# A linear attention that feeds a multiplicative feed-forward block: the first group's x goes straight on chip and its first factors are formed in steps 5 and 6

## The chip, the core and the metric

The kernel runs on one core of a Trainium2 chip. Its engines work side by side, each through its own list of instructions in order, and wait for each other by semaphores: TensorE (PE) multiplies matrices, VectorE (DVE) and ScalarE (ACT) do elementwise work, GpSimd (POOL) small elementwise work and some transfers, SyncE (SP) only issues transfers (DMAs). The metric is the time of one execution on the device in microseconds (us); lower is better.

## The reference

```python
# attention: q, k, v, alpha have the shape (4, 8, 768, 48)
for t in range(S):
    state = alpha[:, :, t, :, None] * state + einsum('bhd,bhe->bhde', k[:, :, t], v[:, :, t])
    y[:, :, t] = einsum('bhd,bhde->bhe', q[:, :, t], state)
x = y.transpose(0, 2, 1, 3).reshape(3072, 384)
# feed-forward: w1, w2 (384, 1024), w3 (1024, 1024), w_out (1024, 384)
out = ((x @ w1) * (x @ w2) @ w3) @ w_out
```

The weights are 64-bit floats in memory and are turned into 32-bit ones on the chip.

## The kernel before

**Two parts.** The first part walks over 24 chunks of 128 positions (4 batches of 6 chunks), one step of the loop `for n in range(N + 1)` for each chunk (L689). The second part (from L787) finishes the feed-forward block. TensorE's products of the feed-forward block (`products`, L515) are put as fill between the attention's work of the first part, and make up nearly all of TensorE's work in the second.

**One step n of the attention.** `load_kq` brings k and q of a later chunk, `load_a` alpha, `load_v` v. `logs` takes the logarithm of alpha, `decays` sums it along the chunk by a product (L340, L343, L346) and takes two exponentials (L349, L350); `decayed` (L359) multiplies k and q by these on VectorE into one of three buffers `qks`. `transposed` turns that with TensorE (L381, an identity matrix as the moving side, 64 rows and 128 columns as weights: two heads of 48 columns, each padded to 64), and ScalarE copies it (L383). `scores` multiplies k and q (L454; from chunk 8 on L430), and VectorE masks the result (L457; L440). `attend_state` (L474) and `attend` (L485, L482) make the chunk's y, which ScalarE copies to `x` (L489); `outer` (L393) and `advance` (L410 to L412, on POOL) carry the state on. In step n the program asks for the scores of chunk n, the transposes of chunk n+1, `attend(n-1)`, `decayed(n+2)` and `decays(n+3)`.

**x on its way to the feed-forward block.** Three chunks make a group of 384 columns, eight groups in all. `attend` puts two stores of x into the queue `later`, and `store` (L305) issues them on SP at the start of the next step, into `xd[g]` in DRAM. `load_x` (L501) reads a group back as `xT` (128 x 3 x 384), and `split_x` makes three parts of it (ScalarE L507, VectorE L508 and L509). For group 0 the load stands in step 4 and the split in step 6.

**Weights.** w1 and w2 come in 128 x 512 pieces (`load_gates`): a load on SP (L236, 512 KB), then the conversion from 64 bits and a split in three parts (L244 to L265), called by `convert` in steps. The first half of the columns takes six pieces, in the order w1, w2, w1, w2, ... The third part of each is formed on TensorE by `third` (L276, L277, L278).

**Gates.** For each group and each 128 of the 1024 columns, `exact` makes the first factor x @ w1 and the second x @ w2 (nine products of 128 x 384 each; L524 and L526 take them out of the result banks), and L563 or L576 multiplies the two. `fill` is a queue of these jobs, and `run(pieces)` calls them between the attention's instructions; one factor is one piece. For group 0 there are eight pieces: five in step 7 and three in step 8.

**What sets the order.** The program's text gives the order for each engine, except that a scheduler may move an instruction of an engine ahead of another that it holds to be later; `after_marks` forbids it to go ahead of the named one. In the order as built, `decayed(n+2)` stands on VectorE ahead of the masks of chunk n in step 4 and ahead of those of chunk 5 in step 5. SP's queue keeps the order of the text. Transfers on it take eight completion semaphores in turn.

**Memory.** `spare` lies in the buffer `x3` that `split_x` writes, and holds alpha of the paired chunks 2 to 7 and two small constant matrices until step 4. `w12` has two tiles, one for each half of the columns.

Of the kernel before, what the change touches and what calls it, by code (L numbers as in the profile page):

```python
# [48 lines left out]
def kernel(  # L49
# [120 lines left out]
    spare = tr[0].tile([C, 3 * KM * TG], FP32R, tag="x3", name="x3")[:].bitcast(FP32)  # L170
    sums2 = spare[:, 0:4 * C].rearrange("p (e s t) -> p e s t", e=2, s=2)
    pairs = [spare[:, ds(4 * C + i * 2 * DM, 2 * DM)].rearrange("p (h s d) -> p h s d", h=H, s=2) for i in range(2)]
# [12 lines left out]

    w12 = [p.tile([C, 3, 2, KM, CW], FP32R, name=f"w12{i}") for i, p in enumerate((w12ap, const))]
# [39 lines left out]
    def to_fp32(*srcs, width=None):  # L226

        n = width or sum(src.shape[1] for src in srcs)
        raw = rawp.tile([C, n], I64, tag="raw", name="raw")
        for i, src in enumerate(srcs):  # L230
            if width:
                rows = ds(i * src.shape[0], src.shape[0])
                to = raw[rows] if len(src.shape) == 2 else raw[rows].rearrange("p (b c) -> p b c", b=src.shape[1])
            else:
                to = raw[:, ds(i * src.shape[1], src.shape[1])]
            nc.sync.dma_start(out=to, in_=src)  # L236
        yield
        words = raw.bitcast(U32).rearrange("p (n w) -> p n w", w=2)
        low, high = words[:, :, 0], words[:, :, 1]

        mant = cvt.tile([C, n], FP32, tag="mant", name="mant")
        top = mant.bitcast(U32)
        rest = cvt.tile([C, n], FP32, tag="rest", name="rest", bufs=2)
        nc.scalar.activation(rest, low, AF.Copy, scale=2.0 ** -52)  # L244
        nc.vector.tensor_scalar(top, high, 0x000FFFFF, 0x00100000, op0=ALU.bitwise_and, op1=ALU.bitwise_or)

        power = cvt.tile([C, n], U32, tag="power", name="power", bufs=2)
        nc.vector.tensor_scalar(power, high, 20, 0x7FF, op0=ALU.logical_shift_right, op1=ALU.bitwise_and)  # L248
        nc.scalar.activation(power, power, AF.Relu, scale=2.0 ** 23, bias=rebias)  # L249
        yield  # L250
        nc.vector.scalar_tensor_tensor(mant, top, 2.0 ** -20, rest, op0=ALU.mult, op1=ALU.add)  # L251
        nc.vector.scalar_tensor_tensor(power, high, 0x80000000, power, op0=ALU.bitwise_and, op1=ALU.bitwise_or)  # L252
        nc.vector.tensor_mul(mant, mant, power.bitcast(FP32))  # L253
        yield
        return mant

    def load_gates(i, kk, half):
        w = yield from to_fp32((moe_w1, moe_w2)[i][ds(kk * C, C), ds(half * CW, CW)])
        h, l, m = (w12[half][:, x, i, kk, :] for x in range(3))
# [110 lines left out]
    def transposed(n):  # L370
# [5 lines left out]
        tp = [bank().rearrange("p (i j c) -> p i j c", i=2, j=NP) for _ in range(2)]  # L376
        for i in range(2):
            for j in range(NP):
                for half in range(2):
                    s = ds(DP * half, DP)  # L380
                    nc.tensor.transpose(tp[half][:, i, j, :], qk[s, i, 2 * j:2 * j + 2, :], ident[s, s])  # L381
        for half in range(2):
            mark["qkT", n] = nc.scalar.copy(qkT[:, :, :, ds(DP * half, DP)], tp[half]).ins  # L383
# [93 lines left out]
    def attend(n):  # L477
# [15 lines left out]
        g, c = divmod(n, G)  # L493
        to = xd[g].rearrange("(b h d) t -> b d h t", b=2, d=D)
        for half in range(2):
            later.append((to[half, :, :, ds(c * C, C)], x[ds(DP * half, D)]))


# [4 lines left out]
    def split_x(g, i):  # L503
        x = st.pop(("xT", g))
# [44 lines left out]
    def factors(g, f):  # L549
        x = [[st["x3", g][:, part, kk, :] for kk in range(KM)] for part in range(3)]  # L550
        half, at = divmod(f * C, CW)
        return [([[w12[half][:, part, i, kk, ds(at, C)] for kk in range(KM)] for part in range(3)], x)
                for i in range(2)]

# [110 lines left out]
    for half in range(DF // CW):  # L665
        for kk in range(KM):
            weights.extend(load_gates(i, kk, half) for i in range(2))
# [17 lines left out]
    FIRST = 6  # L685
# [3 lines left out]
    for n in range(N + 1):  # L689
        store()  # L690
        if n in loads:
            load_x(loads[n])
        if n != 1 and not 2 < n <= FIRST:
            load_a(n + 5)
        raws = (3, 3, 3, 3, 2, 2, 3, 3)[n] if n < 8 else 4
        for m in (n + 3,) * (n <= FIRST) + (n + 4,) * (n >= FIRST):
            load_kq(m)
            if 2 < n <= FIRST and m == n + 3:
                load_a(n + 5)
            if n < FIRST - 2:  # L700
# [17 lines left out]
        if n == FIRST + 1:  # L718
            run(2)
# [3 lines left out]
        if n - 2 in begin and n > FIRST:  # L723
# [3 lines left out]
            fill.extend(gate(g, f) for f in tiles)  # L727
        if n == FIRST:
            with after_marks("l", ("qkT", n + 1)):
                split_x(0, 0)  # L730
            fill.extend(gate(0, f) for f in begin[n - 3][1])
        pieces = ((3, 3, 2, 0) if n > FIRST + 3 else (0, 3, 3, 0))[(n - FIRST) % 4] if n >= FIRST else 0
# [7 lines left out]
        marks = (*[("qkT", n + 1)] * (n < N - 1), *[("qk", n + 1), ("ms", n)] * early, *["x3"] * (n - 2 in begin and n > FIRST))  # L740
        if n < N - 2 and n != FIRST:
# [7 lines left out]
        if n > FIRST:  # L749
# [5 lines left out]
        with after_marks(*[("ms", n)] * (n < 3)):  # L755
            decayed(n + 2)
# [3 lines left out]
        if n == 4:  # L760
            load_x(0)
# [4 lines left out]
        if n <= FIRST:  # L766
# [4 lines left out]
        if n == FIRST:  # L771
            with after_marks("x3", ("e", n + 3)):
                convert(2, raws)
        elif n < N - 2:
            convert(n == FIRST - 1 if early else n % 3 == 0, raws)
        if n == FIRST - 1:
# [97 lines left out]
```

## Time and profile before

| | |
|---|---|
| median of 3 runs | 466.03 us (464.22 to 467.32) |
| profiled execution | 465.8 us, span 464.1 us |
| TensorE busy | 446.0 us, 96% |
| VectorE, ScalarE, GpSimd busy | 371.1 us (80%), 276.3 us (60%), 94.3 us (20%) |
| chain of waits that ends last | PE 87%, DVE 5%, DMA 4%, issue 2%, ACT 1% |
| largest group | L515 `bank<-x,w`, 1152 products, 209.5 us |
| DMA moved | 80.37 MB, 97392 of 148869 packets under 512 bytes |

The span is what the profile's times are measured in; the profiled execution's own time has 1.7 us around it. "Busy" is the time in which an engine works on an instruction; an engine that is not on the chain of waits may be idle at no cost. TensorE's products are pipelined, so one of 337 ns on the page takes about 180 ns of TensorE's time when many follow each other. The chain of waits is followed back from the last instruction, at each step to what released it.

### The profile page before, as it was taken

The numbers are of one execution on the slowest core, as the hardware profiler recorded it, in microseconds if no ns is written. First come the engines' busy times: TensorE is split into PE (matmuls) and PEld (weight loads), VectorE is DVE, ScalarE is ACT, GpSimd is POOL, SyncE is SP. The second block draws the span as 40 slices with busy tenths as digits, with TensorE's granted clock in tenths as the row PEclk, the third lists the DMA queues.
The fourth block names the chain that finished last, engine by engine and source line by source line (L and its number), as shares of the span: only waits on it lengthen the run. The fifth ranks groups of instructions, "written<-read, shape, count | busy, mean of one in ns | idle before, by whom it ended". The sixth has DMA issues, their size and how long they took to land.

```text
span 464.1 us, 11153 instructions
## 1 busy us (share of the span) xinstructions
PE 446.0 (96%) x4296; PEld 424.3 (91%) x4296; DVE 371.1 (80%) x610; ACT 276.3 (60%) x544; POOL 94.3 (20%) x186
## 2 busy tenths in 40 slices
PE   4996999899999999999999999999999999999996
PEld 2674899799999989999999999999999999999996
DVE  2886997999979989899998999997542967776671
ACT  4764984848668553989875776764544543333430
POOL 6332152215322360112221201211110000000000
PEclk9998899999999999999999999999999999999999
DMA  9999999899998965476766446412115966655511
GB/s 174 257 208 235 245 221 206 203 216 230 173 223 178 239 185 154 126 227 211 216 187 204 131 142 177 148 52 86 51 37 153 260 200 180 186 176 162 164 51 52
DMA packets 148869, 80.37 MB, mean 173 GB/s; under 512 B 97392, under 2 KB 138608, under 8 KB 148816
## 3 DMA queue, kind: packets, MB, share of 16 engines
q1 hardware_dynamic: 143040, 64.44, 57.2%
q0 software_dynamic: 5776, 15.22, 10.8%
q8 instruction: 34, 0.56, 0.6%
q14 instruction: 19, 0.16, 0.1%
HBM read 57.58 MB, written 22.06 MB: 172 GB/s over the span
## 4 chain that ended last, share of the span: by engine, by line
PE 87%; DVE 5%; DMA 4%; issue 2%; ACT 1%; SPq 0%; DVEq 0%
PE bank L515 71%; DMA kq<-in_q_dram 4%; PE bank L381 3%; PE bank L430 2%; PE bank L474 2%; PE bank L482 2%; PE bank L454 1%; PE bank L393 1%; PE bank L343 1%; PE bank L346 1%; PE bank L485 1%; PE bank L419 1%; DVE ms L457 1%; DMA ac<-in_alpha_dram 1%; DVE x L509 1%
## 5 line engine op out<-in xcount | busy, mean ns | idle before, releaser
L515 PE MATMUL bank<-x,w 128*128 128x384 f32 x1152 | 209.5, 337 | 1.0 <-DVE ms L440 0.9
L515 PEld LDWEIGHTS bank<-x,w 128*128 128x128 f32 x1152 | 200.2, 188 | 2.8 <-DVE ms L440 1.2
L515 PE MATMUL bank<-w3o,ab 128*128 128x384 f32 x576 | 100.2, 336 | 0.0
L515 PEld LDWEIGHTS bank<-w3o,ab 128*128 128x128 f32 x576 | 99.9, 188 | 0.0
L540 ACT ACTIVATE bank<-bank 128x384 f32<-128x384 f32 x96 | 45.7, 476 | 43.5 <-PE bank L515 43.2
L524 ACT ACTIVATE t<-bank 128x384 f32<-128x384 f32 x64 | 31.6, 495 | 55.1 <-PE bank L515 54.8
L590 POOL DMA_DIRECT2D abd<-ab x45 | 25.8, 573 | 137.7 <-DVE ab L576 121.5
L383 ACT COPY qkT<-bank 128x512 f32<-128x512 f32 x48 | 26.0, 593 | 24.2 <-PE bank L381 24.2
L641 DVE TENSOR_TENSOR ab<-abl,ab 128x1024 fp32r<-128x1024 f32 x24 | 29.4, 1224 | 12.5 <-ACT ab L640 12.5
L640 ACT ACTIVATE ab<-abl 128x1024 fp32r<-128x1024 f32 x24 | 25.5, 1061 | 20.2 <-PE bank L515 18.4
L515 PE MATMUL bank<-wo,w3T 128*128 128x384 f32 x192 | 35.9, 334 | 0.0
L359 DVE TENSOR_TENSOR qk<-kq,e 128x768 f32<-128x768 f32 x24 | 23.2, 966 | 15.4 <-ACT e L350 7.6
L576 DVE TENSOR_TENSOR ab<-bank,r 128x384 f32<-128x384 f32 x44 | 24.2, 550 | 12.5 <-PE bank L515 6.3
L515 PEld LDWEIGHTS bank<-wo,w3T 128*128 128x128 f32 x192 | 33.5, 188 | 0.0
L249 ACT ACTIVATE power<-power,rebias 128x512 uint32<-128x512 uint32 (+1 forms) x36 | 25.1, 698 | 11.2 <-DVE power L248 11.2
L526 DVE SCALAR_TENSOR_TENSOR o<-bank,t 128x384 f32<-128x384 f32 x24 | 13.4, 557 | 22.7 <-issue 13.7
L642 DVE SCALAR_TENSOR_TENSOR ab<-ab,abl 128x1024 fp32r<-128x1024 f32 x24 | 29.2, 1218 | 0.0
L526 DVE SCALAR_TENSOR_TENSOR r<-bank,t 128x384 f32<-128x384 f32 x40 | 22.1, 553 | 6.8 <-ACT t L524 3.4
L251 DVE SCALAR_TENSOR_TENSOR mant<-mant,rest 128x512 f32<-128x512 uint32 (+1 forms) x36 | 23.8, 661 | 3.4 <-ACT rest L244 3.3
L252 DVE SCALAR_TENSOR_TENSOR power<-raw,power 128x512 uint32<-128x512 uint32 (+1 forms) x36 | 23.6, 655 | 2.4 <-ACT power L249 2.4
L253 DVE TENSOR_TENSOR mant<-mant,power 128x512 f32<-128x512 f32 (+1 forms) x36 | 23.6, 656 | 0.5
L244 ACT ACTIVATE rest<-raw 128x512 f32<-128x512 uint32 (+1 forms) x36 | 23.3, 649 | 0.0
(102 smaller groups left out, 675.4 us busy)
## 6 DMA issues: line engine op xcount, KB each, us to landing
abl<-abd SPq DMA_DIRECT2D x24, 512.0 KB, 4.6
abd<-ab POOLq DMA_DIRECT2D x45, 192.0 KB, 3.1
raw<-in_moe_w_dram SPq DMA_DIRECT2D x64, 128.0 KB, 3.4
raw<-in_moe_w_dram SPq DMA_DIRECT2D x12, 512.0 KB, 6.2
xT<-xd POOLq DMA_DIRECT2D x9, 576.0 KB, 4.6
kq<-in_k_dram SPq DMA_DIRECT2D x24, 192.0 KB, 4.9
kq<-in_q_dram SPq DMA_DIRECT2D x24, 192.0 KB, 5.4
xd<-x SPq DMA_DIRECT2D x48, 96.0 KB, 4.0
```

The source lines that it names most:

```text
L249: nc.scalar.activation(power, power, AF.Relu, scale=2.0 ** 23, bias=rebias)
L251: nc.vector.scalar_tensor_tensor(mant, top, 2.0 ** -20, rest, op0=ALU.mult, op1=ALU.add)
L383: mark["qkT", n] = nc.scalar.copy(qkT[:, :, :, ds(DP * half, DP)], tp[half]).ins
L515: nc.tensor.matmul(p, w[part][i], x[part][i], start=start and part == parts[0] and i == 0, stop=stop and part == parts[-1] and i == n - 1, ...
L524: nc.scalar.activation(t, p1, AF.Copy, scale=(1.0 + 1.0 / P) * scale)
L526: nc.vector.scalar_tensor_tensor(to, p2, scale, t, op0=ALU.mult, op1=ALU.add)
L540: nc.scalar.activation(p, p, AF.Copy, scale=1.0 + 1.0 / P)
L576: nc.vector.tensor_mul(ab, p, r[0])
L590: (nc.gpsimd if late else nc.sync).dma_start(out=abd[g][:, f, :], in_=ab)
L640: nc.scalar.activation(t[:, 0], ab, AF.Copy, scale=1.0 - 2.0 ** -13)
L641: nc.vector.tensor_sub(t[:, 1], ab, t[:, 0].bitcast(FP32))
L642: nc.vector.scalar_tensor_tensor(t[:, 2], t[:, 0].bitcast(FP32), -1.0 - 1.0 / P, ab, op0=ALU.mult, op1=ALU.add)
```

## The change

It has five parts. (1) The weights are loaded with w1's three pieces first and then w2's three, and the tile `w12` is cut into four. (2) x of group 0 is not stored to DRAM and read back: `place` writes each chunk by ten transfers on SP, cut where a head crosses a multiple of 128, straight from `x` into `xT`; in steps 2 to 5 `store` stands behind the loads of k, q and alpha; `xT` is stored to `xd[0]` in step 7 for the later visit. (3) The split of group 0 stands in step 5, and its eight factors are two in each of steps 5 to 8: the four first factors (kept in `firsts`, in the place of the last weights), then the four second ones. (4) `decayed` goes to the end of steps 3 to 5, not ahead of the last conversion, and `convert(2)` of steps 1 to 4 goes behind `outer`. (5) `transposed` takes 112 columns of two heads in place of 128, and its copies 112 rows. `spare` moves from `x3` to the place of the last weights.

```diff
+    w12 = {(0, i): w12ap.tile([C, 3, KM, CW], FP32R, name=f"w12{i}") for i in range(2)}
+    w12[1, 0] = const.tile([C, 3, KM, CW], FP32R, name="w12b")
...
+    spare = [last_weights(x, FP32) for x in range(3)]
+    firsts = [spare[2][:, ds(f * TG, TG)] for f in range(CW // C)]
...
+        two_heads = qk.rearrange("p i (j e) d -> p i j (e d)", e=2)
-                    nc.tensor.transpose(tp[half][:, i, j, :], qk[s, i, 2 * j:2 * j + 2, :], ident[s, s])
+                    nc.tensor.transpose(tp[half][0:DP + D, i, j, :], two_heads[s, i, j, 0:DP + D], ident[s, s])
...
         g, c = divmod(n, G)
+        if g == 0:
+            return place(c, x)
...
+    def place(c, x):
+        if ("xT", 0) not in st:
+            st["xT", 0] = xp.tile([C, KM, TG], FP32, tag="xT", name="xT")
+        for h in range(H):
+            half, j = divmod(h, H // 2)
+            f = h * D
+            while f < (h + 1) * D:
+                kk, at = divmod(f, C)
+                n = min(C - at, (h + 1) * D - f)
+                later.append((st["xT", 0][ds(at, n), kk, ds(c * C, C)], x[ds(DP * half + f - h * D, n), j]))
+                f += n
...
+    def first_factor(f):
+        yield from ()
+        exact(firsts[f], *factors(0, f)[0], 1.0)
+
+    def second_factor(f):
+        yield from ()
+        r = gw.tile([C, TG], FP32, tag="r", name="r")
+        exact(r, *factors(0, f)[1], P * P)
+        ab = abp.tile([C, TG], FP32, tag="ab", name="ab")
+        nc.vector.tensor_mul(ab, firsts[f], r)
+        store_ab()
+        st["ab"] = 0, f, ab
...
-        for kk in range(KM):
-            weights.extend(load_gates(i, kk, half) for i in range(2))
+        units = [(i, kk) for i in range(2) for kk in range(KM)]
+        weights.extend(load_gates(i, kk, half) for i, kk in units)
...
-    FIRST = 6
+    FIRST, SOON = 6, 5
...
-        store()
+        if not 1 < n < FIRST:
+            store()
         if n in loads:
             load_x(loads[n])
+        if n == FIRST + 1:
+            nc.sync.dma_start(out=xd[0].rearrange("(k p) t -> p k t", p=C), in_=st["xT", 0])
...
             if 2 < n <= FIRST and m == n + 3:
                 load_a(n + 5)
+            if 1 < n < FIRST:
+                store()
             if n < FIRST - 2:
                 fetch(raws)
...
-        if n == FIRST + 1:
-            run(2)
...
+        if n == SOON:
+            with after_marks(("ms", n), ("qkT", n + 1)):
+                split_x(0, 0)
+            fill.extend(first_factor(f) for f in range(FH))
         if n == FIRST:
-            with after_marks("l", ("qkT", n + 1)):
-                split_x(0, 0)
-            fill.extend(gate(0, f) for f in begin[n - 3][1])
-        pieces = ((3, 3, 2, 0) if n > FIRST + 3 else (0, 3, 3, 0))[(n - FIRST) % 4] if n >= FIRST else 0
+            fill.extend(second_factor(f) for f in range(FH))
+        pieces = ((3, 3, 2, 0) if n > FIRST + 3 else (2, 2, 2, 0))[(n - FIRST) % 4] if n >= FIRST else 2 * (n >= SOON)
...
-        if n < N - 2 and n != FIRST:
+        if n < N - 2 and n != FIRST and not 0 < n < SOON:
             with after_marks(*marks):
                 convert(2 if early else 1, raws)
...
         outer(n)
-        if n > FIRST:
+        if 0 < n < SOON:
+            with after_marks(*marks):
+                convert(2, raws)
+        if n > FIRST or n == SOON:
             third(ready)
...
-        with after_marks(*[("ms", n)] * (n < 3)):
-            decayed(n + 2)
+        if not 2 < n < FIRST:
+            with after_marks(*[("ms", n)] * (n < 3)):
+                decayed(n + 2)
...
-        if n == 4:
-            load_x(0)
...
+        if 2 < n < FIRST:
+            with after_marks("cvt"):
+                decayed(n + 2)
```

## The prediction, as put on record before the changed kernel ran

> **What bounds the kernel now.** I read the page first, then the chain of waits, then windows around its early breaks, then SyncE's (SP's) own timeline. Step n is the loop index of the code, so the sixth step is step 5.
>
> ```profile
> span 464.1 us, 11153 instructions
> ...
> PE 446.0 (96%) x4296; PEld 424.3 (91%) x4296; DVE 371.1 (80%) x610; ACT 276.3 (60%) x544; POOL 94.3 (20%) x186
> ...
> PE   4996999899999999999999999999999999999996
> ...
> DMA  9999999899998965476766446412115966655511
> ```
>
> TensorE (PE) is busy 96% of the span; its slices fall short only at the start, once near slice 7 and at the very end. So the end is PE's work plus the few places where PE stands. From 186 us on the chain is one piece of products, and nothing here changes that part. DMA is full over the first eight slices (93 us).
>
> The chain of waits (start, duration, what) shows the one large break after the first microseconds:
>
> ```profile
> 34.62 7.67 DMA kq<-in_q_dram
> 42.37 0.47 issue
> 42.84 0.25 DVE qk L359
> 43.09 0.62 issue
> 43.71 0.70 DVE ms L457
> 44.45 0.80 PE bank L276
> ...
> 69.28 0.60 PE bank L474 x16
> ```
>
> VectorE (DVE) takes its work in order. `decayed(6)` (L359) stands before the masks of step 4 (L457) and waits for q of chunk 6, which SP issued at 34.62 and which lands at 42.29. DVE is idle 4.20 us, PE 3.59 us (40.86 to 44.45). The last line is where step 8 begins on PE, my mark for comparing: by then PE has done 45 of the products L515.
>
> ```profile
> 30.72:43.32 12.60, 9.52 (x138) 7.13 (x134) 8.03 (x14) 7.88 (x17) 4.43 (x8) 1.00 1.18 239
> 43.32:50.15 6.83, 5.70 (x56) 4.60 (x58) 6.80 (x13) 3.36 (x7) 1.99 (x3) 0.50 0.98 217
> 50.15:57.00 6.85, 6.85 (x102) 5.42 (x99) 6.19 (x11) 6.57 (x15) 0.50 (x1) 1.00 1.20 260
> ```
>
> In these windows (length, then busy time by engine, granted clock, DMA share) PE's clock is 0.50 from 43.32 to 50.15: it falls 2.46 us after PE stopped and returns 5.7 us after PE resumed. The cost of that is 44.45 to 50.15 at half rate, 2.85 us. The stall and its echo together are 3.59 + 2.85 = 6.4 us, the most that removing this break can bring.
>
> ```profile
> 28.01 1.91 SPq L305 DMA_DIRECT2D xd<-x  x2
> 30.02 0.39 SPq L153 DMA_DIRECT2D kq<-in_k_dram  x1
> 30.46 0.78 SPq L154 DMA_DIRECT2D kq<-in_q_dram  x1
> 31.34 1.74 SPq L236 DMA_DIRECT2D raw<-in_moe_w_dram  x1
> ...
> 45.94 0.37 SPq L501 DMA_DIRECT2D xT<-xd  x1
> ```
>
> SP's timeline: its transfers follow each other without a pause. Two small ones back to back start 0.42 us (28.01, 28.43) to 0.48 us (46.40, 46.88) apart; longer ones wait for room in the queue. The landings show the service: q of chunk 5 at 35.40, raw weights 1.54 us after the transfer before them, each k or q some 0.9 us.
>
> **The change, part by part.** Sum against the profiled execution: 465.8 us, of which 464.1 are span; the median of the runs is 466.03, 0.2 above it.
>
> *Masks ahead of decay.* In steps 3 to 5 `decayed` goes behind the conversions, and in the order as built ms(4) stands before qk(6). Walking the engines from 35 us with the rows' durations: tmp 0.3 and three conversion operations 0.6 each (the power row of ScalarE, ACT, in between) end at 37.5; qk(5) 0.9 at 38.4; masks 1.2 at 39.6; then 0.6, 0.7, 0.3, 1.9 (with ACT's power at 42.2) to 43.4, qk(6) 44.3. PE: transposes of chunk 5 38.4 to 39.0, attend 1.0, outer 0.5, decays 1.4, third 0.5, so 42.4; step 5: state 0.6, scores 1.1 (44.1), transposes 44.3 to 44.9, attend 1.0, third 0.5: **46.4**. Before, this work and decays of 0.84 end at 52.15. The stall of 3.59 us is gone.
>
> *Work now put at that point.* Step 5 then wants 18 products on x of group 0 and before that the split (ACT L507, DVE L508 and L509), whose rows are
>
> ```profile
> 55.85 1.22 ACT L507 ACTIVATE x<-xT 128x1152 fp32r<-128x1152 f32 x1
> ```
>
> ```profile
> 57.42 1.35 DVE L508 TENSOR_TENSOR x<-xT,x 128x1152 fp32r<-128x1152 f32 x1
> 58.68 1.35 DVE L509 SCALAR_TENSOR_TENSOR x<-x,xT 128x1152 fp32r<-128x1152 f32 x1
> ```
>
> So the question is when x of group 0 lies in `xT`. Before it went through DRAM (six stores, one load at 45.94, landed 50.71). Now it is thirty pieces of 8 to 24 KB on SP, ten in each of steps 2, 3 and 4, behind k, q and alpha of the step. With the store of `xT` that step 7 adds, SP issues 31 in place of 7: 24 more at 0.45 us, 10.8 us of its queue. The store stands ahead of that step's loads, which have some 7 us to spare (q of chunk 11 landed at 71.13, used at 77.97).
>
> *The wait that this adds.* In the program as built SP's transfers take eight completion semaphores in turn, so each waits until the eighth before it has landed. In the trace before at most seven others are outstanding and room in the queue is what holds SP; ten small pieces behind big ones make the count decide. k(5) and q(5) are issued by 31.0 (31.24 before, two stores were ahead) and land at 33.9 and 34.8 (35.40 less two stores of 0.3). The seventh and eighth piece wait for them, the tenth goes at 35.65. Raw weights go at 36.1 and land 1.9 + 1.5 later (1.9 us is what a 96 KB store takes on a quiet queue at 186.5; the six output rows at the end take 1.8 to 1.9), k, q and alpha 0.9 each behind: 36.1 + 3.4 + 2.7 = 42.2. The fifth to eighth piece of chunk 1 wait for just these four, so the tenth goes at 42.2 + 0.9 = 43.1 or, with v of POOL between (0.9), 43.6; the next round is 7.5 later: raw at 44.0, alpha landed 50.1, tenth piece of chunk 2 at 51.0, landed 52.9. I take **xT complete at 53**. From below: if the count never decides, SP issues 37 transfers from 31.0 at 0.45, 47.7 + 1.9 = 49.6. From above: pieces land as stores on the full queue do, 4.4 to 5.5 us instead of 1.9: 51.0 + 5 = 56. I take the middle because SP's bursts empty the queue behind them.
>
> *Who stands behind it.* PE has nothing else in order from 46.4. ACT's split ends at 53 + 1.3 = 54.3, DVE's two at 56.9; DVE, which waits from 45.5, has queued behind them 0.6 + 0.7 + 0.55 + 1.2 + 0.55 + 0.6 and qk(7) 0.9: 62.0. The transposes of step 6 need qk(7); PE's scores are done by then (part 2 of the first factor 57.5, second 59.2, decays 0.84, state 0.6, scores 1.1: 61.7). From 62.0 PE has transposes 0.6, attend 1.0, outer 0.45, 18 products 3.3, decays 0.84, two thirds 0.94, scores 1.1, transposes 0.6, attend 1.0, outer 0.45, 18 products 3.3, decays 0.35: 13.9, so step 8 begins at 75.9, with 54 products done. Before: 69.28 with 45, and nine more at 0.185 are 1.67: 70.9. **Difference +5.0 us**; it is zero for xT at 48.0, +1.6 at 49.6, +8 at 56. Steps 5 to 8 hold 72 products as before, so from step 9 on the two are alike.
>
> *Clock.* PE stands 46.4 to 54.3, 7.9 us, longer than the 3.59 that halved the clock. If it returns 5.7 us after resuming, at 60.0, the first factors start at half rate; until 58 that hides behind the split, then some five products take 0.185 more each: **+1.0** (0 if the clock is back by 58, 2.7 if not before 63). The Trainium skill, *TensorE: Matmul & The Clock Gate*, section on the HAM clock gate, lets some 3.4 us of sustained work bring the clock back; here it took 5.7. By the page the term is 0 and the sum 1.0 less.
>
> *Transposes of 112 columns* (L381, 16 in each of 24 steps). Sixteen take 0.50 to 0.64 us with 128-column weights; L393 with 64 columns takes 0.45. For 16 of those 64 columns that is a quarter of 0.05 to 0.19, times 24: 0.3 to 1.1, and 0 is the other end since the two lines differ in more. I take **-0.7**. The same page, section on LDWEIGHTS, makes the load proportional to columns, 16 / 1.2 = 13 ns on each of 384 loads; an estimate from it, halves of the array side by side, is -2.6, and the sum would be +3.4.
>
> *At nothing:* w1 ahead of w2 (same raw transfers, same places in the queues; the six are done by the end of step 5, and step 5 needs w1 alone; uncovered it would be one more conversion, 3.1 us of DVE); first factors kept (same copies and products; their place is written again only by the last weights, after step 14); the spare buffers moved.
>
> Sum: 5.0 + 1.0 - 0.7 = +5.3, 465.8 + 5.3 = 471.1; on the median 471.3. I say 471.
>
> **Rivals.** *Not slower: only issue time counts.* The pieces go out at 0.45 us and are short on the rings; xT at 49.6 gives +1.6 + 1.0 - 0.7 = +1.9, 468. For it: small raw pieces late in part 1 went out with up to seven outstanding at 0.47 us. Against: the built waits. The total is xT - 48 + 0.3, so this case holds for xT below 52.4 (1% is 4.66).
> *Faster: the stall goes and no new one comes.* Place: PE's order in step 5; if the pieces pass the big transfers on the rings and xT is complete before 48, each further microsecond is a gain, up to 43.5, where PE's products (46.4) no longer wait: -4.5 - 0.7, 461 on the median. For it: chunk 2 of x is copied by 36.4 and could move at once. Against it: 37 issues alone end at 47.7.
> *Worse: full-queue latencies* on every piece, as the upper bound has it: xT at 56, +8 + 0.3, 474. That is also the case in which the change doesn't do what it says, for the split would then start no sooner than its 55.85 of before, while the products that wait for it stand two steps earlier in PE's order.
>
> **How the numbers follow.** Slower by over 1%, as worked out (0.40) or worse (0.12): xT after 52.4. Within 1%, the issue-only case and what lies around it: 0.33. Faster by over 1%: 0.15, more than the 37 issues allow, because the walk above is a chain of some twenty waits, each with an error of its own. 1% is 461.4 to 470.7, about what a measurement of this kernel can tell from no change. The forecast's own range is 469 to 475; the whole one goes from half way between the issue-only case and the faster one to somewhat above the full-queue one (2.7 of clock in place of 1.0, no gain from the columns): 463 to 477.
>
> **What would show it.** Right: no wait of DVE on q before the masks of step 4; PE standing some 8 us between the third of step 5 and the first products, released by ACT's split; the split by the pieces' landing near 53; SP's pieces with pauses of 0.8 to 1 us at the fifth to eighth of each ten; a second half-clock window near 50 to 60. Wrong: a split before 49, pieces issued evenly at 0.45, or a break of PE in step 6 or 7 that is none of these.

## Result and the profile after

The changed kernel takes 480.96 us (median of 4 runs, 480.19 to 482.66) against 465.75 (464.22 to 467.32) of the kernel before on the same chip: 1.0338 of it, 95% interval 1.0298 to 1.0377. The forecast was 471.0 with a range of 463 to 477: the side was right, the size was not, and the range did not hold it. The profiled execution has a span of 479.3 us, 15.2 more than the one before.

The page of the changed kernel (busy time of the engines, then PE's busy tenths and granted clock in 40 slices of 12 us):

```profile
PE 449.1 (94%) x4296; PEld 425.2 (89%) x4296; DVE 372.8 (78%) x610; ACT 277.7 (58%) x544; POOL 98.3 (21%) x186
...
PE   4996279999999999999999999999999999999996
PEclk9999669999999999999999999999999999999999
```

PE is busy 3 us more: the granted clock is at half from 47.33 to 50.75 and from 54.16 to 67.81 us, before it was from 43.32 to 50.15. The other 12.1 of the 15.2 us are more idle time of PE, and that is the length of one hole, in slices 5 and 6 (48 to 72 us). PE's own timeline (start, duration, what, in brackets the idle time before it and what ended it) shows the hole with its edges:

```profile
47.17 1.00 PE L393 MATMUL bank<-ident,qk 64*112 64x64 f32 x16 [3.35 <-ACT la L335]
...
50.60 0.47 PE L288 MATMUL bank<-w,signs 128*128 128x512 f32 x1
63.15 5.95 PE L541 MATMUL bank<-x,w 128*128 128x384 f32 x18 [12.08 <-ACT x L533]
...
84.95 0.67 PE L486 MATMUL bank<-qkT,T 48*64 48x128 f32 x16
```

The wait of step 4's third for the masks is gone. PE ends the third of step 5 at 51.07 and then stands 12.08 us for ScalarE's split of x. The last line is the start of step 8, the prediction's mark: 84.95 where 70.9 is the like point of before. That is 14.05 of the 15.2 us; the other 1.2 come after step 8.

The chain of waits names what the split waits for:

```profile
59.24 0.59 SPq L316
59.87 1.81 DMA xT<-x
61.94 1.17 ACT x L533
```

SP's issue of the last piece at 59.87, its landing at 61.68, the split. So T, the landing of x, is 61.7 where the prediction has 53. SP's timeline shows what it did until then; nothing on it is idle:

```profile
28.22 9.31 SPq L316 DMA_DIRECT2D xT<-x  x10
...
38.87 2.06 SPq L154 DMA_DIRECT2D kq<-in_q_dram  x1
40.98 2.58 SPq L147 DMA_DIRECT2D ac<-in_alpha_dram  x1
...
54.08 6.39 SPq L316 DMA_DIRECT2D xT<-x  x10
```

Ten pieces take 9.31 us of SP in the first round, 6.63 (from 43.66) in the second and 6.39 in the third. Singly they start 0.63 us apart (59.24 and 59.87 in the chain above), whether they have 16, 32 or 48 rows; the prediction has 0.45. The first of a ten took 3.62, 0.93 and 0.68 us, and q and alpha of the second round 2.06 and 2.58.

### The profile page after: what moved, and what is told of

Its sections match the earlier page's. It is cut to its first block, busy times and chain, and to the rows that moved or that the text cites. A ratio compares the mean times of both kernels' runs of the same rounds, so it can differ in the third digit from the quotient of the medians.

```text
span 479.3 us, 11186 instructions
## 1 busy us (share of the span) xinstructions
PE 449.1 (94%) x4296; PEld 425.2 (89%) x4296; DVE 372.8 (78%) x610; ACT 277.7 (58%) x544; POOL 98.3 (21%) x186
## 4 chain that ended last, share of the span: by engine, by line
PE 86%; DVE 4%; DMA 3%; ACT 2%; SPq 2%; issue 1%; ACTq 0%; DVEq 0%
PE bank L541 70%; PE bank L442 3%; PE bank L393 3%; SPq L316 2%; PE bank L486 2%; PE bank L494 2%; PE bank L405 1%; PE bank L466 1%; DMA raw<-in_moe_w_dram 1%; PE bank L357 1%; PE bank L354 1%; PE bank L351 1%; DVE qk L370 1%; PE bank L431 1%; DMA kq<-in_k_dram 1%
## 5 line engine op out<-in xcount | busy, mean ns | idle before, releaser
L541 PE MATMUL bank<-x,w 128*128 128x384 f32 x576 | 110.2, 344 | 14.2 <-ACT x L533 12.1
L541 PEld LDWEIGHTS bank<-x,w 128*128 128x128 f32 x576 | 100.8, 191 | 18.3 <-ACT x L533 12.6
L566 ACT ACTIVATE bank<-bank 128x384 f32<-128x384 f32 x96 | 45.8, 478 | 43.8 <-PE bank L541 43.6
L541 PE MATMUL bank<-x,w12b 128*128 128x384 f32 x288 | 56.4, 338 | 0.0
L541 PE MATMUL bank<-x,w12c 128*128 128x384 f32 x288 | 56.3, 338 | 0.0
L541 PEld LDWEIGHTS bank<-x,w12c 128*128 128x128 f32 x288 | 51.1, 188 | 0.0
L541 PEld LDWEIGHTS bank<-x,w12b 128*128 128x128 f32 x288 | 51.1, 188 | 0.0
L395 ACT COPY qkT<-bank 112x512 f32<-112x512 f32 x48 | 25.8, 590 | 23.7 <-PE bank L393 23.7
L534 DVE TENSOR_TENSOR x<-xT,x 128x1152 fp32r<-128x1152 f32 x14 | 18.9, 1352 | 16.6 <-ACT x L533 16.4
```

What stands on the lines that cost most here:

```text
L395: mark["qkT", n] = nc.scalar.copy(qkT[0:DP + D, :, :, ds(DP * half, DP)], tp[half][0:DP + D]).ins
L534: nc.vector.tensor_sub(t[:, 1], x, t[:, 0].bitcast(FP32))
L541: nc.tensor.matmul(p, w[part][i], x[part][i], start=start and part == parts[0] and i == 0, stop=stop and part == parts[-1] and i == n - 1, ...
L566: nc.scalar.activation(p, p, AF.Copy, scale=1.0 + 1.0 / P)
```

## Experiments

All times below are medians, with the ratio to the kernel before on the same chip. Two theories stood at the start: the landing T alone sets the time, and T is late because SP pays for each transfer. The rivals: the early split, the raw weights or the clock are what is paid for; or the pieces are slow on their way rather than at the queue.

### Does T set the time?

**six_pieces**: each chunk in six pieces of 64 rows.

```diff
-        for h in range(H):
-            ...
-                later.append((st["xT", 0][ds(at, n), kk, ds(c * C, C)], x[ds(DP * half + f - h * D, n), j]))
+        for i in range(2 * KM):
+            half, j = divmod(i, KM)
+            kk, at = divmod(i * DP, C)
+            later.append((st["xT", 0][ds(at, DP), kk, ds(c * C, C)], x[ds(DP * half, DP), j]))
```

> The changed kernel with x of a chunk moved in six pieces of 64 rows instead of ten of 8 to 48 rows, so 18 instead of 30 (they put x of group 0 in a wrong order of rows, so the experts of group 0 work on other numbers; the work is the same). Theory (the queue's price is one of 0.63 us for each transfer, whatever its size, and the landing T of the last piece sets the time one for one): twelve transfers fewer are 7.6 us, T goes from 61.7 to 54.1, the time from 481.0 to 473.4, 1.017 of before. Rival A (the price follows the rows or bytes, 64 rows cost 1.0 us): T stays at 61 to 62 and the time at 480 to 481. Rival B (T does not set the end): T falls as the theory says, the time by less than 3 us.

Measured: 474.91 us, 1.0212 (1.0174 to 1.025). T is 55.86, 5.8 sooner, and the span 473.2, 6.1 less. The 64-row pieces start 0.63 to 0.64 apart, so a piece's price does not follow its rows, and rival A falls; rival B falls too. T did not come the whole 7.6 forward: in round 2 alpha and the first two pieces held SP longer (3.18, 1.82 and 1.56 us; in the changed kernel 2.58, 0.93 and 0.54).

**x_through_dram**: two stores for each chunk and one load, as before, the split still in step 5.

```diff
-        if g == 0:
-            return place(c, x)
...
+        if n == 4:
+            load_x(0)
```

> The changed kernel with x of group 0 through DRAM as before (two stores for each chunk on SP, one load in step 4, no pieces and no store of x in step 7), the split still in step 5 and all else as changed. Theory: SP has 24 transfers fewer, so x lies in xT at 49 to 52 in place of 61.7, and the time is 61.7 - T lower: 468 to 471. Rival (products in step 5 are too early for any way to bring x, or the other edits cost): above 475. Second rival (the masks' order alone is worth its 6.4 us and x is early enough): 465 or less.

Measured: 473.65, 1.019 (1.0162 to 1.0218). T is 54.20, later than the 49 to 52 expected, since the load waited until chunk 2's stores had landed (50.0). The time is lower by what T is sooner, so the theory's rule holds and its T does not. With no piece at all the early split costs 7.9 us of span, for x is late on this way as well.

**raw_first**: `fetch(raws)` ahead of `store()` in steps 2 and 3.

```diff
+            if n < FIRST - 2:
+                fetch(raws)
             if 1 < n < FIRST:
                 store()
-            if n < FIRST - 2:
-                fetch(raws)
```

> The changed kernel with the raw weights of steps 2 and 3 issued ahead of the ten pieces instead of behind them. In the changed kernel VectorE and then PE waited 3.05 and 3.35 us at 43 to 47 for raw weights that SP issued behind the first ten pieces. Theory (those waits are covered, since PE stands for x afterwards anyway and x's landing T sets the time): T stays within 1 us of 61.7 and the time within 1 us of 481. Rival (the late raw weights are part of the loss): 476 to 478.

Measured: 480.80, 1.0336 (1.0305 to 1.0368), T 60.95. The numbers are the theory's, but the edit moved nothing: `fetch` issues a load only while fewer than three pieces of weights are begun, and it issued none at the new place. SP's timeline has its transfers in the same order as in the changed kernel, with the raw weights still behind the ten pieces, and PE's wait is still there:

```profile
29.51 7.17 SPq L316 DMA_DIRECT2D xT<-x  x10
36.78 0.53 SPq L247 DMA_DIRECT2D raw<-in_moe_w_dram  x1
```

```profile
46.64 1.10 PE L393 MATMUL bank<-ident,qk 64*112 64x64 f32 x16 [3.44 <-DVE qk L370]
```

So this run is the changed kernel once more, and says nothing of the raw weights. Two others do. In six_pieces the wait at this place is nearly gone (long_rows, below, has 0.23):

```profile
44.15 0.66 PE L393 MATMUL bank<-ident,qk 64*112 64x64 f32 x16 [0.21 <-DVE qk L370]
```

PE is through with the third of step 5 at 46.5 there, not at 51.07, and yet the span ends as long after T (next table). So the 3.35 us that PE waits at 43.8 to 47.2 are covered by the later wait for x.

**last_chunk_only**: chunks 0 and 1 through DRAM, pieces for chunk 2 alone.

```diff
-        if g == 0:
+        if g == 0 and c == G - 1:
             return place(c, x)
...
+            if n == 4:
+                nc.sync.dma_start(out=st["xT", 0][:, :, 0:2 * C], in_=xd[0].rearrange("(k p) t -> p k t", p=C)[:, :, 0:2 * C])
```

> The changed kernel with only the last chunk of group 0 moved in ten pieces; the first two go through DRAM with two stores each and one load of 384 KB in step 4. Theory (SP's 0.63 us for each on-chip piece and the queue's fullness set T): ten pieces from about 45.5 end at 52, landed at 53.5 to 54, no sooner than the 54.2 of x through DRAM: T at 53 to 55, time 472 to 474. Rival (the queue is short enough that the pieces go at once behind their copies): T at 50, 469.

Measured: 472.90, 1.0169 (1.0137 to 1.0201), as the theory has it, with T 52.20 a little sooner (its profiled execution, 471.05, was the shortest of four). Its chain of waits holds a line that the next part needs:

```profile
43.94 5.89 DMA xT<-x
...
49.84 0.51 SPq L316
```

With two runs of the next part, seven kernels in which PE stands for the landing of x in step 5 can be set side by side:

| kernel | T, us | profiled span, us | span - T |
|---|---|---|---|
| last_chunk_only | 52.20 | 469.3 | 417.1 |
| x_through_dram | 54.20 | 472.0 | 417.8 |
| long_rows | 54.73 | 472.9 | 418.2 |
| six_pieces | 55.86 | 473.2 | 417.3 |
| raw_first | 60.95 | 478.3 | 417.4 |
| changed kernel | 61.68 | 479.3 | 417.6 |
| pieces_to_dram | 63.54 | 481.7 | 418.2 |

Over 11 us of T the difference stays within 1.1. As long as PE stands for that landing, the time follows T one for one, however x arrives. A span of 464.1 would need T near 46.4. Two kernels further down have the split in step 5 and do not stand for the landing, and they lie off this line: pieces_by_pool (T 55.46, span 476.4), where PE waits for GpSimd, and x_at_once (T 36.1, span 463.5).

### Why is T so late?

**pieces_to_dram**: the same ten pieces, written to `xd[0]`, and one load behind them.

```diff
-                later.append((st["xT", 0][ds(at, n), kk, ds(c * C, C)], x[...]))
+                later.append((xd[0][ds(f, n), ds(c * C, C)], x[ds(DP * half + f - h * D, n), j]))
...
+        if n == 4:
+            load_x(0)
```

> The changed kernel with the ten pieces of a chunk written to DRAM (and one load of x in step 4 behind them, as before) instead of to xT on chip; pieces of the same size. It asks what sets the 0.63 us of a piece. Theory (a transfer with one row of 512 bytes for each partition costs 0.63 whatever its target): pieces 0.63 apart, the last landed at about 62, the load 4 us more, T at 66, 484 to 486. Rival (the target on chip costs it; stores of 192 rows to DRAM go out in 0.43): pieces at 0.43 to 0.45, the last landed at 56, T at 60, 478 to 480.

Measured: 483.25, 1.04 (1.0378 to 1.0423), T 63.54. The time is near the theory's and the price is the rival's: the same pieces, with DRAM as target, start 0.46 us apart instead of 0.63. SP's third ten, 6.39 above, is

```profile
51.74 5.16 SPq L316 DMA_DIRECT2D xd<-x  x10
```

and the last piece is issued 3.4 us sooner than in the changed kernel, at 56.5. That is less than thirty times 0.17, 5.1, because alpha of the second round then held SP 4.30 us in place of 2.58. The load of x takes the gain back and more (issued 58.67, 4.87 us).

**long_rows**: k, q and alpha between the pieces come in rows of 1536 bytes.

```diff
+        if 5 <= n <= 7 and src is not v or 8 <= n <= 9 and src is alpha:
+            return src[b].rearrange("h s d -> (h s) d")[0:C * H].rearrange("(p h) d -> p h d", h=H)
```

> The changed kernel with k and q of chunks 5 to 7 and alpha of chunks 8 and 9 (those that SP issues between the pieces) taken from other, contiguous rows: the same bytes in rows of 1536 bytes instead of eight of 192 for each partition (so those chunks work on other numbers). In the changed kernel q, alpha and the first piece of each ten took 1.9 to 3.6 us of SP instead of some 0.6. Theory (SP is held because many short rows fill its queue; that time stands in series with ten pieces of 0.63): these holds go, SP's round is ten by 0.63 and four by 0.45, 8.1 us, the last piece is issued near 52, T at 53 to 55, 5 to 7 us sooner than 61.6, and the time as much lower, 474 to 476. Rival (the bytes behind them hold it, or the eighth transfer before has to land): T above 58, 477 or more.

Measured: 474.11, 1.0201 (1.0141 to 1.0261), T 54.73, 6.95 sooner, as the theory has it. The bytes are the same, and q and alpha of the second round on SP's timeline are

```profile
36.27 0.42 SPq L156 DMA_DIRECT2D kq<-in_q_dram  x1
36.74 0.42 SPq L149 DMA_DIRECT2D ac<-in_alpha_dram  x1
```

They take 0.42 where they took 2.06 and 2.58. So it is the number of rows, not of bytes, that held SP: k, q and alpha bring 1024 rows of 192 bytes each. Their service is not what became faster: k, q and alpha of this round land 1.54 and 0.69 us after one another, in the changed kernel 0.95 and 0.58. I read the hold as a queue with room for so many rows, where an issue that finds the earlier ones unserved lasts until some are served; no row of a profile shows the room itself. The tenth piece of the second ten now goes out at 44.1, where the prediction has 43.6.

This run also shows the wait on which the prediction was built, and so does last_chunk_only. Above, SP issues a piece at 49.84, 0.01 us after the piece eight transfers before it has landed (43.94 + 5.89 = 49.83). In long_rows the seventh piece of the second ten starts 1.54 us after the sixth, 0.02 after q, eight before it, has landed at 42.23. In the changed kernel no transfer of SP between 25 and 65 us starts within 0.1 us of such a landing: SP comes to each later than that.

### Other ways to pay

**split_later**: the pieces stay, the split and the products go back to steps 6 to 8.

```diff
-        if n == SOON:
-            with after_marks(("ms", n), ("qkT", n + 1)):
+        if n == FIRST + 1:
+            run(2)
+        if n == FIRST:
+            with after_marks("l", ("qkT", n + 1)):
                 split_x(0, 0)
...
-        pieces = ((3, 3, 2, 0) if n > FIRST + 3 else (2, 2, 2, 0))[(n - FIRST) % 4] if n >= FIRST else 2 * (n >= SOON)
+        pieces = ((3, 3, 2, 0) if n > FIRST + 3 else (0, 3, 3, 0))[(n - FIRST) % 4] if n >= FIRST else 0
```

> The changed kernel with the split of x of group 0 back in step 6 and its products back in steps 7 and 8, as before; the thirty pieces, the masks ahead of the decay and the rest stay. Theory (the loss is that PE's order holds products on x in step 5, ahead of step 6, while x lands at 61.7): with the products in step 7 only the part of the wait that is left over counts; before had PE at step 7's products from about 62, so the loss of 15 us shrinks to 0 to 3 us, less what the order of the masks brings: 463 to 468. Rival (the SP queue itself makes k, q, alpha and raw weights late, by up to 15 us, whoever uses x): the time stays at 476 or more.

Measured: 479.94, 1.0346 (1.0289 to 1.0404). The theory fell, and the time is the rival's. PE waits for no x, and loses as much:

```profile
58.29 1.10 PE L393 MATMUL bank<-ident,qk 64*112 64x64 f32 x16 [5.24 <-DVE qk L370]
70.42 1.10 PE L393 MATMUL bank<-ident,qk 64*112 64x64 f32 x16 [4.27 <-ACT rest L255]
```

The transposes of step 6 (and those of step 5, 3.22 us) wait behind raw weights that SP issued after the pieces: VectorE stands 5.82 us for those of step 6. Those of step 7 have two waits that end together, raw weights issued at 64.78 and VectorE's split of x with the decay behind it (to 70.27). The pieces with the late split cost 14.5 us of span, the early split alone 7.9 (x_through_dram), both together 15.2, all against the first profile of before, an execution 1.6 us longer than the median of before in these runs (464.21). Each hides behind the other, so undoing the one leaves the other's cost.

**pieces_by_pool**: GpSimd issues the pieces inside `place`.

```diff
-                later.append((st["xT", 0][ds(at, n), kk, ds(c * C, C)], x[ds(DP * half + f - h * D, n), j]))
+                nc.gpsimd.dma_start(out=st["xT", 0][ds(at, n), kk, ds(c * C, C)], in_=x[ds(DP * half + f - h * D, n), j])
```

> The changed kernel with the thirty pieces issued by GpSimd (POOL) as soon as x of a chunk is formed, instead of by SP behind k, q and alpha. Theory (SP's queue of 0.63 us for each transfer is the whole loss): SP's raw weights come some 4 to 6 us earlier in each step, the last piece lands at 46 to 52, the time is 465 to 471. Rival (the pieces are slow as such, on the rings or at their destination): T after 57, the time above 476. Second rival: POOL's own work (decay and v) gets late behind its thirty issues of about 1 us each, and a wait on v or the decay takes the place of the wait on x: 472 to 480 with PE idle elsewhere.

Measured: 477.11, 1.0265 (1.0233 to 1.0298): the second rival. Thirty issues at 0.50 us each stand between POOL's decay and v, nine of them wait besides until the eighth transfer before them has landed (they start 0.28 us after it), and PE stands where it never did:

```profile
37.33 1.13 PE L486 MATMUL bank<-qkT,T 48*64 48x128 f32 x16 [7.24 <-POOL T L424]
```

### Where is the gain of taking the stall away?

**masks_first**: the kernel before with part 4 of the change alone.

```diff
-        if n < N - 2 and n != FIRST:
+        if n < N - 2 and n != FIRST and not 0 < n < 5:
...
+        if 0 < n < 5:
+            with after_marks(*marks):
+                convert(2, raws)
...
-        with after_marks(*[("ms", n)] * (n < 3)):
-            decayed(n + 2)
+        if not 2 < n < FIRST:
+            with after_marks(*[("ms", n)] * (n < 3)):
+                decayed(n + 2)
...
+        if 2 < n < FIRST:
+            with after_marks("cvt"):
+                decayed(n + 2)
```

> The kernel before with one edit: in steps 3 to 5 the decay goes behind the conversions, so the masks of step 4 do not wait for q of chunk 6. Theory (the prediction's figure: stall 3.59 and half clock 2.85 are gone): up to 6.4 us, 457.8 at best; with PE at step 5's third at 48.0 where x through DRAM showed it, some 3.5 us, 461. Rival (PE waits for the split of x at 57.4 to 60 all the same, since x's load at 45.94 does not move): 463 to 465.

**columns**: the kernel before with part 5 alone.

```diff
-                    nc.tensor.transpose(tp[half][:, i, j, :], qk[s, i, 2 * j:2 * j + 2, :], ident[s, s])
+                    nc.tensor.transpose(tp[half][0:DP + D, i, j, :], two_heads[s, i, j, 0:DP + D], ident[s, s])
```

> The kernel before with one edit: the transposes of q and k load 112 columns instead of 128 and the copy takes 112 partitions. The prediction has -0.7; sixteen of them took 0.61 to 0.66 in the changed kernel where they took 0.66 to 0.71 before, 0.05 by 24 steps is 1.2: 463 to 463.6, 0.997 to 0.999 of before. Rival (the page's estimate of 13 ns on each of 384 loads): -2.6, 461.6, 0.9945. Second rival (the copies to three quarters of the partitions or the grouping cost something): above 464.5.

Measured: 463.98, 0.9997 (0.9978 to 1.0017), and 464.41, 1.0006 (0.9986 to 1.0026), 12 runs each. Neither moves the time. The -0.7 of the columns (0.9985) lies at the edge of what these runs leave open; the -2.6 worked out from the page is outside, though the weight loads themselves took less, 130 ns for 139 (medians of 384). masks_first has the number of its rival but not the reason: PE goes into the first products at 56.81 without a wait for the split. In masks_first's profile stall and half clock are gone (span 461.3, clock 1.0), yet its runs spread as those of before do, 463.1 to 466.6 against 463.0 to 466.6.

**before_again** and **before_third**: the kernel before, profiled twice more.

> The kernel before once more, for a second profile of it. The prediction's sum starts from the stall of 3.59 us and the half clock after it in one execution of 465.8 us, and masks_first, which has neither, had the same median. Theory (the stall is not in each execution): here PE's idle time at step 4's third is under 2 us, the clock another, and the time 463 to 464. Rival (it is in each execution, and masks_first gives its gain back later): idle of 3 us or more there and a time near 465.

> The kernel before a third time, with the same question as the second: theory, the idle time at step 4's third differs from the 3.59 us of the first profile by over 1.5 us and the time goes with it; rival, it is there each time.

Measured: 465.29 and 463.81. PE's timeline in the second profile, at the place that had [3.59 <-DVE ms L457] in the first:

```profile
42.20 0.50 PE L276 MATMUL bank<-w,signs 128*128 128x512 f32 x1 [1.64 <-DVE ms L457]
...
43.76 1.13 PE L474 MATMUL bank<-qkT,T 48*64 48x128 f32 x16 [0.83 <-POOL T L412]
```

The third has 1.66 and 0.84. So a stall is there each time, here at half the size, as the theory has it; the time of the second profile, 465.29, is the rival's, so it doesn't go with the stall alone. A second wait stands right behind the first: POOL's T, at the end of POOL's own chain of small transfers. With the masks' wait gone, PE meets that one. masks_first's profile has that wait too (0.34, state at 42.50). It also has waits that before_again has nowhere, for the decay that now stands behind the conversions: 0.60 us in step 4 and, in steps 5 and 6,

```profile
45.78 0.71 PE L381 MATMUL bank<-ident,qk 64*128 64x64 f32 x16 [1.52 <-DVE qk L359]
...
51.33 0.72 PE L381 MATMUL bank<-ident,qk 64*128 64x64 f32 x16 [0.81 <-DVE qk L359]
```

VectorE itself stands 2.13 us for T ahead of that decay. So part 4 gives a part of the stall back in the next steps. masks_first ends the third of step 5 at 48.83, before_again at 51.31 and before_third at 50.65; step 8 begins at 66.87, only 0.8 to 1.4 sooner than in these two, not 2.4 as against the first profile. 0.8 of 464 is 0.2%, what its interval leaves open. The stall of 3.59 us was that of one execution on the long side; the half clock behind it, 6.83 us long, is the same in all three.

**neither**: x through DRAM and the split in step 6, the rest of the change kept.

```diff
-        if g == 0:
-            return place(c, x)
...
-        if n == SOON:
+        if n == FIRST:
...
-        pieces = (... else (2, 2, 2, 0))[(n - FIRST) % 4] if n >= FIRST else 2 * (n >= SOON)
+        pieces = (... else (0, 3, 3, 0))[(n - FIRST) % 4] if n >= FIRST else 0
```

> The fourth cell of the square: x of group 0 through DRAM and the split in step 6, as before, with the rest of the change (masks ahead of the decay, columns, weights' order, first factors kept). The other three cells have 7.9 us for the early split alone, 14.5 for the pieces alone and 15.2 for both over the span of before. Theory (the rest of the change is worth what removes the stall at 40.86, 3 to 6.4 us, and 0.7 to 1.2 for the columns): 457 to 460.5, 0.985 to 0.992 of before. Rival (the stall only moves: DVE meets the next late landing at once): 463 to 465.

Measured: 467.73, 1.0073 (1.0053 to 1.0093), slower than both expectations. Three second factors fell into step 8, and VectorE waited for the store of the first to give its buffer back:

```profile
82.97 0.56 DVE L588 TENSOR_TENSOR ab<-w12c,r 128x384 f32<-128x384 f32 x1 [4.97 <-DMA abd<-ab]
```

**neither_spread**: the same with first and second factors in turn.

```diff
-            fill.extend(first_factor(f) for f in range(FH))
-            fill.extend(second_factor(f) for f in range(FH))
+            for f in range(FH):
+                fill.extend((first_factor(f), second_factor(f)))
```

> The kernel called neither, with first and second factors of a tile formed in turn (first, second, first, second) instead of four firsts and then four seconds. There, three second factors fell into step 8, their three products were stored one behind the other at 77.67, and VectorE waited 4.97 us for the third buffer. Theory (that wait and its half clock are the whole of its 0.7%): 463 to 465, no different from before, so that weights' order, kept factors, masks and columns together are worth nothing. Rival (something else of the rest costs): 467 or more.

Measured: 465.63, ratio 1.0000 (0.9973 to 1.0028; before had 464.67 on the same chip), and no such wait, as the theory has it. Order of the weights, kept factors, masks and columns are together worth nothing that can be measured.

**x_at_once**: the changed kernel with xT there by 36 us, from one load of other data.

```diff
         if g == 0:
-            return place(c, x)
+            return
...
+            if n == 2:
+                st["xT", 0] = xp.tile([C, KM, TG], FP32, tag="xT", name="xT")
+                nc.sync.dma_start(out=st["xT", 0].rearrange("p k t -> p (k t)"), in_=v[3, 0:4].rearrange("h (p s) d -> (h p) (s d)", p=C // 4))
```

> The changed kernel without its thirty pieces: xT is filled by one load of 576 KB of other data (rows of v) in step 2, the same bytes in one transfer, so the products of group 0 work on other numbers. It asks what the products in step 5 would be worth if x came in time. Theory (the time is set by T, the landing of x, and by nothing else of the change): T lies before 43.5, PE goes from the third of step 5 straight into the products, and the prediction's lower bound for the change holds, 4.5 and 0.7 below before: 459 to 460. Rival (the break of before is filled by the next late landing, as masks_first alone showed, whose median did not move): 463 to 465. Second rival (the products in step 5 cost something of their own, on PE's or ACT's order): 466 or more.

Measured: 465.89, 1.0025 (1.0003 to 1.0047), between the two rivals; the theory fell. With x there at 36.1 the early split costs 0.5% at most, and brings nothing. PE is at the products at 46.94, close to the 46.4 of the prediction, and then waits for the three parts of the split one by one:

```profile
47.51 0.79 PE L541 MATMUL bank<-x,w 128*128 128x384 f32 x3 [0.58 <-ACT x L533]
48.91 0.79 PE L541 MATMUL bank<-x,w 128*128 128x384 f32 x3 [0.60 <-DVE x L534]
50.27 3.89 PE L541 MATMUL bank<-x,w 128*128 128x384 f32 x12 [0.58 <-DVE x L535]
...
70.01 0.67 PE L486 MATMUL bank<-qkT,T 48*64 48x128 f32 x16
```

The clock is at half from 50.26 to 53.67. From 46.94 the first 18 products take 7.2 us where 18 take 3.33 elsewhere: 3.9 of the 4.5 us that the prediction gives this case go there. Step 8 begins at 70.01; the like points of before's second and third profile (68.31 and 67.66, and 1.67 for nine products) are 69.98 and 69.33. The order that the change sets up had no gain to give here, even with x free.

## Why the prediction was wrong

- *Bound and mechanism*: right. The stall of step 4 goes, PE then stands for x between the third of step 5 and the first products, and what ends the wait is ScalarE's split behind the last piece's landing.
- *From T to the time*: right. The prediction has step 8 at T + 22.9 and 1.0 for the clock; it was at T + 23.3 (61.68 and 84.95). By T - 48 + 0.3 a landing of 61.68 gives 464.1 + 14.0 = 478.1 of span; 479.3 was measured. With the right T the rule is 1.2 short. That part lies after step 8, where the prediction holds the two kernels alike; the spread of single executions is as large, and the -0.7 of the columns, which is in the rule, was not seen in the runs.
- *T*: the step that failed. 53 predicted, 61.7 measured, 8.7 of the 9.9 us by which the span was missed. The last piece was to be issued at 51.0 and was at 59.87; its flight of 1.9 was right (1.81). Two terms of the walk along SP's queue were wrong. A piece costs SP 0.63 us, not the 0.45 of stores to DRAM (pieces_to_dram: 3.4 us of the last issue). And k, q and alpha, with the first piece behind them, hold SP 1.9 to 3.6 us at a time; the walk put that at nothing, let the pieces go out right behind alpha and wait only for landings (long_rows: 6.95 us of T). With that hold gone, and at 0.63 a piece, T is 54.73, within 2 us of the forecast, and it is then the landings that SP waits for, as the prediction has it. The two are not simply added, since a cheaper piece lets the next alpha wait longer.
- *The eight outstanding transfers*: a real wait (last_chunk_only and long_rows show it to 0.02 us, pieces_by_pool on GpSimd's queue to 0.28) that did not decide here: between 25 and 65 us SP came to each transfer at least 1.18 us after the eighth before it had landed. The prediction took "count" and "room and issue" as alternatives, the larger of which decides. Here they stood one behind the other: issue time and hold were paid in each round, and the count then found its transfer landed. The pauses of 0.8 to 1 us that were named as a sign did not come; the evenly spaced pieces that were named as a sign of failure did, at 0.63 instead of 0.45.
- *PE at 46.4*: late, 51.07, for raw weights issued behind ten pieces (a wait of 3.35 us) and a half clock after it. It cost nothing: six_pieces and long_rows have PE there at 46.5 and the same distance from T to the end.
- *Clock*: about right. The half clock lasted from 54.16 to 67.81, and the first 18 products took 5.95 us where 18 take 3.33. But a part of the 2.6 hides behind the split, as the prediction said: without a clock term it has these products end at T + 6.2, and they ended at T + 7.4, which is +1.2 against its +1.0. The Trainium skill, *TensorE: Matmul & The Clock Gate*, section on the HAM clock gate, has a free-running window of 3413 ns; the stretches at half rate seen here agree: 3.41 us (x_at_once), 6.83 (before), 10.24 (six_pieces), 13.65 (the changed kernel), 17.07 (pieces_to_dram) and 20.48 (raw_first), one to six windows. How long the clock stayed at half after PE had resumed differed from run to run, 3.8 us in six_pieces, 5.7 in the kernel before, 7.0 in x_through_dram; the prediction took the one 5.7 that it had, and its other value, 0 by the page, did not come.
- *The gain*: the rival with 461 had its condition, T below 43.5, fulfilled in x_at_once, and its price did not come. The order paid 3.9 us for the parts of the split and the half clock in that run, and the stall of other executions is shorter. The 6.4 us were the most that one execution could show; in the median the masks alone brought 0.0 with 0.2% either way. The wait for POOL's T (before_again) and the waits for the decay put back (masks_first) fit that, but neither was taken away in a run, so what holds the gain back is argued and not shown.
- *At nothing*: right for weights' order and kept factors as far as neither_spread shows, which has the masks and the columns with them, as long as no three products are stored in one step (neither, 0.7%).

## What to carry to other kernels

When loads are cut into pieces, count the issuing queue first: pieces times the issue time of that very kind of transfer, plus what large transfers with many short rows hold it for, in series; one number from a transfer to another place is not enough. A wait that ends a stall in one profile should be looked at in a second profile of the same kernel before its whole length is put down as a gain. Whether an edit moved what it was to move is read from the timeline and not from the time (raw_first). And before work is moved earlier, one run with its data there for free tells what the move can bring at most; here that was nothing.

## What the runs showed of the hardware

- SP's issue of a piece from chip memory to chip memory took 0.63 us from start to start, for 16 to 64 rows of 512 bytes; the same piece to DRAM 0.46. The raw-weight transfer right behind the pieces took 0.53 us of SP in the one and 0.37 in the other, so the price may not be the piece's alone; what makes it is not settled. GpSimd's issue took 0.50.
- The same bytes of q and alpha took 2.06 and 2.58 us of SP as 1024 rows of 192 bytes, and 0.42 as 128 rows of 1536 bytes, behind others of their kind.
- The stretches at half clock were 3.41 us or two to six times that long.
- The weight load of a transpose took 139 ns with 128 columns and 130 with 112 (medians), and the time of the kernel did not move.
